# Four attention layers on one core: VectorE's share of the exponentials gets its own storage from the first layer's end on

## The chip, the core and the metric

The kernel runs on one core of a Trainium2 chip. The metric is the device time of one execution in microseconds (us). TensorE (PE) multiplies matrices, ScalarE (ACT) computes exponentials, VectorE (DVE) does elementwise work, GpSimd (POOL) masks and issues some transfers, SyncE (SP) issues the other transfers.

## The reference

Four residual attention layers run one after the other on a 2048 x 640 activation, with 32 heads of 20 columns. Layers 0 and 2 use a causal window of 256 keys; layers 1 and 3 attend to all 2048 keys.

```
def _layernorm(x, axis=-1, eps=1e-5):
    m = jnp.mean(x, axis=axis, keepdims=True)
    v = jnp.var(x, axis=axis, keepdims=True)
    return (x - m) / jnp.sqrt(v + eps)
...
        scores = jnp.einsum("bhqd,bhkd->bhqk", q, k) * (Dh ** -0.5)
        p = _softmax(scores, axis=-1)
        o = jnp.einsum("bhqk,bhkd->bhqd", p, v)
        return (lambda x, *d: x.transpose(*d))(o, 0, 2, 1, 3).reshape(B, S, D) @ wo
...
    x = x + _A_ref(_layernorm(x, axis=-1), A_wqkv, A_wo)
    x = x + _B_ref(_layernorm(x, axis=-1), B_wqkv, B_wo)
    x = x + _A_ref(_layernorm(x, axis=-1), A_wqkv, A_wo)
    x = x + _B_ref(_layernorm(x, axis=-1), B_wqkv, B_wo)
    return x
```

## The kernel before

The 2048 rows are four chunks of 512 (`NC`, `C`), the 32 heads are eight groups of four (`G`). A unit of work, `Unit(l, c, g, part)`, is one layer, one chunk of queries, one group of heads, and in some cases only a part of the keys. A full-attention unit over all keys has 64 banks: one bank is the scores of one head against 128 keys for 512 queries, 128x512 in one PSUM bank. Chunk 0 of layer 1 is cut into four parts of the keys, chunk 0 of layer 3 into two (`PARTS`): a unit of a quarter has 16 banks, a unit of three quarters has 48. Parts exist because the later keys are not yet there: the last chunks of the layer below are still being computed. Their sums wait in `part_o`, the tile `raw_o`, until the last part adds its own (`finish_unit`, L863).

The units stand in one fixed list, `units`, in which layers overlap: windowed units of layer 0 alternate with layer 1's parts 0 to 1, windowed units of layer 2 stand between units of layer 1's chunks 1 to 3 and of layer 3's chunk 0. Part 2 of layer 1's chunk 0 (keys 8 to 12 in units of 128) begins after the last windowed unit of layer 0.

The main loop makes one round (`t`) after the other. A round takes two or three banks from the list (`next_tile`), lets PE write their scores into one of two sets of PSUM banks (L1416), and lets ACT take the exponential of all of them in one instruction (L1442) into one of six `pt` tiles. Two to three rounds later PE multiplies them with the values into the one bank `op` (L1475). At the end of a unit VectorE moves `op` away (`finish_unit`), and the values of the next unit follow.

Everything else, normalisation, projections, output projection, is the background: generators in `todo`, advanced by `background` and `pump` between the rounds. They share one or two PSUM banks (`take_m`), which VectorE empties (`evac`, L334, L339). `keep_clock` fills a round with products of `masks` and `ident` that nobody reads (L315).

VectorE computes some of the exponentials itself. `side_giver` (L932) looks for a full-attention unit among the current and the next two, whose tensors are loaded, and `side_take` (L955) takes two banks off its end. Until chunk 1 of layer 3 a round then holds two banks for ACT and one for VectorE. `side_fixed` (L975) reads that bank into an integer tile `xi`; after two of them, `chain` (L997) computes the exponential of the pair in steps: `fraction` (L1005), `square` (L1013), `cubic` (L1017) and `whole` (L1023), the last two in halves of 512 columns where `HALF` applies. `side_work` emits a step when the planner's own measure of VectorE's backlog, `state["lag"]`, allows it (`WORK_1` 1.4 in layer 1, `WORK` 2.2 later). PE multiplies the result with the values before the unit ends (`side_values`, L1057); at a unit's end `side_ready` can put the end off for up to five rounds, and `side_done` makes what is still missing (`side_push`).

The chain needs two `xi` tiles, one `t` tile and a few tiles for results (`side["out"]`). Before the change there are two periods. `side_early` puts all of them into `raw_o`, when this is free: from layer 1's chunk 1 on, until layer 3 needs `raw_o` again. `side_start` takes three of the five normed-row tiles (`xtp`, tile name `xnT`) and parts of `ka` and `qa` (the windowed layers' keys and queries) after the last windowed unit, from group 4 of layer 3's chunk 0 on. `xnT` holds the transposed normalised rows of one chunk; its other users are the projections.

Of the kernel before, what the change touches and what calls it, by code (L numbers as in the profile page):

```python
# [9 lines left out]
BF16 = mybir.dt.bfloat16  # L10
# [34 lines left out]
PRE_1 = 0.8  # L45
KEEP = 30
HALF = True
HALF_3 = False
MOST_1 = 64
GAP_1 = 5  # L50
QA = 4

# [7 lines left out]
def kernel(  # L60
# [21 lines left out]
    vap = pool("vap", 10)  # L82
    xtp = pool("xtp", 5)
    onp = pool("onp", 2)
# [29 lines left out]
    ka_all = big.tile([P, KA, C], BF16, name="ka", tag="ka")  # L114
    kas = [ka_all[:, n, :] for n in range(KA)]
    qa_all = big.tile([P, QA, C], BF16, name="qa", tag="qa")
    qas = [qa_all[:, n, :] for n in range(QA)]
# [209 lines left out]
    users = {}  # L327

    def used(l, c):
        users[l, c] -= 1  # L330
        if users[l, c] == 0:
            live["xnT"] -= 1

    def evac(out_, in_):  # L334
# [75 lines left out]
    def t_ln(l, c):  # L410
# [18 lines left out]
        )  # L429
        xt = xtp.tile([P, KD, C], BF16, name="xnT", tag="xnT")  # L430

# [431 lines left out]
    def finish_unit(u):  # L863
        l, c, g = u.l, u.c, u.g
        state["lag"] += 0.7
        if u.part and u.part[1] < NT:
            if not part_o:
# [19 lines left out]
        if u.part:  # L887
            nc.vector.tensor_tensor(out=oT, in0=part_o["t"][:, g, :], in1=op, op=ALU.add)
        else:
            nc.vector.tensor_copy(out=oT, in_=op)  # L890
# [8 lines left out]
    side = {  # L899
        "xi": deque(), "chain": deque(), "out": deque(), "late": False, "early": False,  # L900
        "half": None, "at": 0, "last": 0,
    }
    givers = [u for u in units if not u.windowed and (u.l, u.c) != (1, 0)]

    def side_tiles(xi, t, outs):

        side["xi"].extend(xi)
        side["t"] = t
        side["out"].extend(outs)

    def side_start():

        assert live["xnT"] <= 2 and not side["chain"] and side["half"] is None
        tl = [xtp.tile([P, KD, C], BF16, name="xnT", tag="xnT") for _ in range(3)]
        live["xnT"] += 3
        f = [v[:, 0:4, :].rearrange("p a b -> p (a b)").bitcast(F32) for v in tl]
        side["xi"].clear()
        side["out"].clear()
        outs = [ka_all[:, KA - 6 + 2 * n : KA - 4 + 2 * n, :] for n in range(3)]
        outs += [qa_all[:, 2 * n : 2 * n + 2, :] for n in range(2)]  # L920
        side_tiles(f[0:2], f[2].bitcast(F16)[:, 0 : 2 * C], outs)
        side["late"] = True

    def side_early():

        b = part_o["t"]
        f = [b[:, 2 * n : 2 * n + 2, :].rearrange("p a b -> p (a b)") for n in range(2)]
        outs = [b[:, n, :].bitcast(BF16).rearrange("p (a b) -> p a b", a=2) for n in range(5, G)]
        side_tiles(f, b[:, 4, :].bitcast(F16), outs)
        side["early"] = True  # L930

    def side_giver():  # L932

        if not side["late"] and state["tick"] < side["last"] + GAP_1:
            return None
        if side["half"] is not None:
            return side["half"][0]
        if not side["xi"]:
            return None
        while side["at"] < len(givers) and not givers[side["at"]].rest:  # L940
            side["at"] += 1
        for n in range(side["at"], min(side["at"] + 3, len(givers))):
            u = givers[n]
            if id(u) not in loaded or state["tick"] < loaded[id(u)] + 8:
                return None
            if not side["late" if u.l == 3 else "early"]:
                return None
# [49 lines left out]
    def chain(u, xi):  # L997
# [23 lines left out]
        def whole(h):  # L1021
# [5 lines left out]
            if h.stop == 2 * C:  # L1027
                side["xi"].append(xi)
# [28 lines left out]
    def side_values(u, wait):  # L1057

        pairs = side_out.get(id(u), ())
        while u.valued < len(pairs) and pairs[u.valued][1] + wait <= state["tick"]:  # L1060
            pt = pairs[u.valued][0]
            for i in range(2):
# [5 lines left out]
                )  # L1068
            side["out"].append(pt)
            u.valued += 1  # L1070
# [165 lines left out]
    def first_ln():  # L1236

        users[0, 0] = 9
        live["xnT"] += 1
        xt = xtp.tile([P, KD, C], BF16, name="xnT", tag="xnT")  # L1240

# [54 lines left out]
    with tc.manual_schedule():  # L1296
# [74 lines left out]
        while ended is None or t < ended + 8:  # L1371
# [203 lines left out]
```

## Time and profile before

| | us |
|---|---|
| median of three runs | 2171.07 (2169.65 to 2171.41) |
| the profiled execution | 2167.19 |
| its span, first to last instruction | 2165.5 |
| ACT busy | 2086.1 |
| PE busy | 1924.8 |
| VectorE busy | 1488.7 |
| GpSimd busy | 485.9 |
| exponentials on ACT: 128x1536 / 128x1024 | 1280 / 280 instructions |
| banks that VectorE's chain takes (rows of L989) | 210 + 112 = 322 |

The profiled execution took 2167.19 us, 1.7 us more than its span, and 3.9 us less than the median of the three runs. Busy times are sums over the span. PE's busy time holds the unread products too. Stages of the list stand in the span as follows, found from the order of the rounds: layer 1's chunk 0, part 2, from 373.1 to 435.3 us and part 3 to 492.7; chunks 1, 2 and 3 to 744.9, 1005.1 and 1269.1; layer 3's chunk 0, first part, to 1487.7 and second to 1542.6; its chunks 1 to 3 to the end.

### The profile page before, as it was taken

What the parts mean: (1) busy time and instruction counts of PE and PEld (TensorE: products, weight loads), DVE (VectorE), ACT (ScalarE), POOL (GpSimd) and SP (SyncE); (2) the same over time, 40 slices, a digit from 0 to 9 for tenths busy, and PEclk for the clock granted to TensorE, in tenths of its full rate; (3) what the DMA queues carried; (4) which work ended last, traced back from release to release, by engine and by line L of the source; (5) the groups of instructions that cost most, each with busy time, mean ns of one, the idle gap of its engine ahead of it and who ended that gap; (6) DMA issues with size and microseconds to landing.
All of it is one profiled execution on the core that took longest, in us unless ns stands there. A gap on an engine that the chain in (4) does not pass through costs nothing. (4 is left out here: it accounts for less than half of the span.)

```text
span 2165.5 us, 73279 instructions
## 1 busy us (share of the span) xinstructions
PE 1924.8 (89%) x31759; PEld 754.6 (35%) x31759; DVE 1488.7 (69%) x2625; ACT 2086.1 (96%) x1717; POOL 485.9 (22%) x953
## 2 busy tenths in 40 slices
PE   8999999988889898888988989888898898888898
PEld 4444443433333333333333433332332222222222
DVE  5656665426666776776767733676779887888896
ACT  7889899999999999999999999989999999999997
POOL 6665546110122113410053112511000000000000
PEclk9999999999999999999999999999999999999999
DMA  6223233322211323112241133112121111111100
GB/s 204 76 84 107 75 92 101 81 80 64 79 45 27 84 61 90 41 41 61 56 112 33 37 86 99 39 42 77 53 60 44 35 36 42 32 33 39 42 30 17
DMA packets 88418, 137.29 MB, mean 63 GB/s; under 512 B 20766, under 2 KB 63486, under 8 KB 88094
## 3 DMA queue, kind: packets, MB, share of 16 engines
q1 hardware_dynamic: 68878, 79.43, 13.9%
q0 software_dynamic: 19216, 53.17, 8.3%
q8 instruction: 249, 4.08, 0.8%
q14 instruction: 75, 0.61, 0.1%
HBM read 99.52 MB, written 27.79 MB: 59 GB/s over the span
## 5 line engine op out<-in xcount | busy, mean ns | idle before, releaser
L1442 ACT ACTIVATE pt<-ps 128x1536 bf16<-128x1536 f32 (+2 forms) x1641 | 2051.7, 1406 | 46.4 <-PE ps L1416 35.5
L1416 PE MATMUL ps<-qt,kt 32*128 32x512 bf16 x3914 | 544.6, 383 | 59.8 <-ACT pt L1442 52.5
L315 PE MATMUL ps<-masks,ident 128*32 128x512 bf16 x5652 | 505.6, 384 | 96.6 <-ACT pt L1442 47.5
L1475 PE MATMUL ps<-pt,vt 128*21 128x512 bf16 x3774 | 375.9, 386 | 1.8 <-issue 1.0
L1416 PEld LDWEIGHTS <-kt 32*128 32x128 bf16 x3914 | 154.7, 91 | 460.2 <-issue 440.4
L315 PEld LDWEIGHTS <-ident 128*32 128x32 bf16 x5652 | 180.3, 94 | 278.9 <-issue 253.5
L1515 POOL TENSOR_SCALAR_AFFINE_SELECT pt<-pt 128x256 bf16<-128x256 bf16 (+2 forms) x506 | 217.1, 451 | 187.6 <-ACT pt L1442 175.3
L315 PE MATMUL ps<-xnT,wqk 128*32 128x512 bf16 x3320 | 225.2, 381 | 11.9 <-DMA wqk<-in_B_wqkv_dram 2.1
L339 DVE CAST st<-ps 128x512 bf16<-128x512 f32 x134 | 92.5, 690 | 143.9 <-PE ps L315 143.6
L1475 PEld LDWEIGHTS <-vt 128*21 128x21 bf16 x3774 | 93.4, 89 | 260.1 <-issue 256.3
L989 DVE TENSOR_SCALAR xnT<-ps 128x512 int32<-128x512 f32 x210 | 144.1, 687 | 34.6 <-PE ps L971 27.5
L315 PE MATMUL ps<-wop,on 128*32 128x320 bf16 x3712 | 160.5, 300 | 5.7 <-DVE x_sb L587 3.9
L1526 DVE TENSOR_TENSOR pt<-pt,masks 128x256 bf16<-128x256 bf16 (+3 forms) x268 | 113.4, 438 | 46.5 <-ACT pt L1442 44.3
L315 PEld LDWEIGHTS <-on 128*32 128x32 bf16 x5760 | 122.3, 95 | 63.7 <-issue 29.8
L1416 PE MATMUL ps<-qa,ka 32*128 32x384 bf16 (+2 forms) x1408 | 118.0, 276 | 22.5 <-ACT pt L1442 19.1
L587 DVE TENSOR_TENSOR x_sb<-x_sb,ps 128x320 bf16<-128x320 bf16 x120 | 58.2, 485 | 101.6 <-PE ps L315 101.1
L1185 DVE TENSOR_TENSOR on<-on,ps 128x512 bf16<-128x512 bf16 x128 | 86.4, 684 | 59.2 <-PE ps L315 57.0
L315 PE MATMUL ps<-wv,xnT 128*32 128x320 bf16 x2560 | 116.0, 301 | 9.0 <-DVE vs L339 2.0
L315 PEld LDWEIGHTS <-wqk 128*32 128x32 bf16 x3320 | 83.2, 96 | 96.0 <-issue 38.1
L989 DVE TENSOR_SCALAR raw_o<-ps 128x512 int32<-128x512 f32 x112 | 76.8, 686 | 47.3 <-PE ps L1416 46.8
L890 DVE CAST on<-ps 128x512 bf16<-128x512 f32 x112 | 76.7, 685 | 37.9 <-PE ps L1475 30.7
L554 POOL DMA_DIRECT2D k_d<-st x75 | 42.5, 567 | 225.7 <-DVE st L339 213.0
(99 smaller groups left out, 1797.9 us busy)
## 6 DMA issues: line engine op xcount, KB each, us to landing
vt<-v_d SPq DMA_DIRECT2D x48, 336.0 KB
kt<-k_d SPq DMA_DIRECT2D x192, 80.0 KB
wqk<-in_B_wqkv_dram POOLq DMA_DIRECT2D x80, 160.0 KB, 3.5
wqk<-in_A_wqkv_dram POOLq DMA_DIRECT2D x70, 160.0 KB, 3.6
k_d<-st POOLq DMA_DIRECT2D x75, 128.0 KB, 2.5
q_d<-st POOLq DMA_DIRECT2D x75, 128.0 KB, 2.3
qt<-q_d SPq DMA_DIRECT2D x384, 20.0 KB
v_d<-vs POOLq DMA_DIRECT2D x16, 336.0 KB, 3.0
```

What stands on the lines that cost most here:

```text
L315: nc.tensor.matmul(out_[r], lhsT=lhsT[:, r], rhs=rhs, start=start, stop=stop)
L339: nc.vector.tensor_copy(out=out_, in_=in_)
L554: nc.gpsimd.dma_start(out=dst, in_=staging.pop())
L587: nc.vector.tensor_tensor(out=xv, in0=had, in1=yp, op=ALU.add)
L890: nc.vector.tensor_copy(out=oT, in_=op)
L989: nc.vector.tensor_scalar(out=xi.bitcast(I32)[:, i * C : (i + 1) * C], in0=z, scalar1=SCALE * LOG2E * FIX, scalar2=127.5 * FIX, op0=ALU.mu ...
L1185: nc.vector.tensor_tensor(out=oT, in0=oT, in1=zb, op=ALU.mult)
L1416: nc.tensor.matmul(sp[:, i, col * P : (col + qn) * P], lhsT=u.k(kc, j), rhs=u.q(j, q0, qn), start=True, stop=True,)
L1442: nc.scalar.activation(out=pt[:, i:k, b0 * P :], in_=sp[:, i:k, b0 * P :], func=ACT.Exp, scale=SCALE,)
L1475: nc.tensor.matmul(op[32 * j : 32 * j + VW, q0 * P : (q0 + qn) * P], lhsT=u.v(kc, j), rhs=pg[:, i, col * P : (col + qn) * P], start=(first ...
L1515: nc.gpsimd.affine_select(out=v, in_=v, compare_op=ALU.is_gt if later else ALU.is_ge, fill=0.0, base=0, pattern=[[0, k - i], [-1 if later ...
L1526: nc.vector.tensor_tensor(out=pt_[:, i:k, cols], in0=pt_[:, i:k, cols], in1=mv_, op=ALU.mult)
```

## The change

The five normed-row tiles become one tile, `xt_all`, with a list of free places. When part 2 of layer 1's chunk 0 has begun and places 2 to 4 are free, `side_first` keeps these three for the chain for the rest of the kernel: two `xi`, one `t` and two result tiles. Two places are left for normed rows. From the end of layer 1's chunk 0 `raw_o` is lent as eight further result tiles (`side_lend`) and withdrawn when layer 3 begins (`side_retire`, `side_home`); `ka` and `qa` are added after the last windowed unit as before (`side_start`).

The chain therefore no longer pauses between its two periods. Chunk 0 of layer 1 may give banks too (`givers`), in parts 2 and 3, and so may chunk 0 of layer 3 from its first group on. Before chunk 1 of layer 1, a taken bank may follow the last after three rounds (`GAP_0`), not five (`GAP_1`), and the backlog limit there is 2.2, not 1.4. Units of 16 banks may give five rounds after their load (`AFTER`), not eight. The halves of 512 columns apply until `side_start`, not by layer.

```
+AFTER = 5
 HALF = True
+FROM = 2
...
+GAP_0 = 3
...
-    xtp = pool("xtp", 5)
...
+    xt_all = big.tile([P, 5, KD, C], BF16, name="xnT", tag="xnT")
...
+    xt_free = deque(range(5))
+    xt_n = {}
+
+    def take_xt(l, c):
+
+        xt_n[l, c] = xt_free.popleft()
+        return xt_all[:, xt_n[l, c]]
+
     def used(l, c):
         users[l, c] -= 1
         if users[l, c] == 0:
             live["xnT"] -= 1
+            xt_free.append(xt_n.pop((l, c)))
...
-        xt = xtp.tile([P, KD, C], BF16, name="xnT", tag="xnT")
+        xt = take_xt(l, c)
...
             nc.vector.tensor_tensor(out=oT, in0=part_o["t"][:, g, :], in1=op, op=ALU.add)
+            if l == 1 and g == G - 1:
+                side_lend()
...
-    givers = [u for u in units if not u.windowed and (u.l, u.c) != (1, 0)]
...
+    givers = [u for u in units if not u.windowed]
+    away = []
+
+    def side_home(kind, v):
+
+        if any(v is a for a in away):
+            away[:] = [a for a in away if a is not v]
+        else:
+            side[kind].append(v)
+
+    def side_retire(parts):
+
+        for v in parts:
+            for kind in ("xi", "out"):
+                if any(v is a for a in side[kind]):
+                    side[kind] = deque(a for a in side[kind] if a is not v)
+                    break
+            else:
+                away.append(v)
+
+    def side_first():
+
+        for n in range(2, 5):
+            xt_free.remove(n)
+        live["xnT"] += 3
+        f = xt_all[:, 2:5].rearrange("p n a b -> p (n a b)")
+        f = [f[:, n * 2 * C : (n + 1) * 2 * C] for n in range(7)]
+        b = xt_all[:, 2:5].rearrange("p n a b -> p (n a b)")
+        outs = [f[n].rearrange("p (a b) -> p a b", a=2) for n in (5, 6)]
+        side["xi"].extend(b[:, 4 * n * C : 4 * (n + 1) * C].bitcast(F32) for n in range(2))
+        side["t"] = f[4].bitcast(F16)
         side["out"].extend(outs)
+        side["on"] = True
+
+    def side_lend():
+
+        b = part_o["t"]
+        side["lent"] = [b[:, n, :].bitcast(BF16).rearrange("p (a b) -> p a b", a=2) for n in range(G)]
+        side["out"].extend(side["lent"])
 
     def side_start():
 
-        assert live["xnT"] <= 2 and not side["chain"] and side["half"] is None
-        tl = [xtp.tile([P, KD, C], BF16, name="xnT", tag="xnT") for _ in range(3)]
-        live["xnT"] += 3
...
-        side["xi"].clear()
-        side["out"].clear()
         outs = [ka_all[:, KA - 6 + 2 * n : KA - 4 + 2 * n, :] for n in range(3)]
         outs += [qa_all[:, 2 * n : 2 * n + 2, :] for n in range(2)]
-        side_tiles(f[0:2], f[2].bitcast(F16)[:, 0 : 2 * C], outs)
+        side["out"].extend(outs)
         side["late"] = True
 
-    def side_early():
...
     def side_giver():
 
-        if not side["late"] and state["tick"] < side["last"] + GAP_1:
+        gap = GAP_0 if state["unit"] < index[1, 1, 0, None] else GAP_1
+        if not side["late"] and state["tick"] < side["last"] + gap:
             return None
...
-            if id(u) not in loaded or state["tick"] < loaded[id(u)] + 8:
-                return None
-            if not side["late" if u.l == 3 else "early"]:
+            if id(u) not in loaded or state["tick"] < loaded[id(u)] + (AFTER if u.size == 16 else 8):
                 return None
...
-        halves = (slice(0, C), slice(C, 2 * C)) if HALF and (u.l == 1 or HALF_3) else every
+        halves = (slice(0, C), slice(C, 2 * C)) if HALF and not side["late"] else every
...
-            limit = WORK if side["late"] else WORK_1
+            limit = WORK if side["late"] or state["unit"] < index[1, 1, 0, None] else WORK_1
...
-                if not side["early"] and state["unit"] >= index[1, 1, 0, None]:
-                    side_early()
+                if (
+                    not side["on"] and state["unit"] >= index[1, 0, 0, PARTS[1][FROM]]
+                    and all(n in xt_free for n in range(2, 5)) and live["xnT"] <= 2
+                ):
+                    side_first()
+                if side["lent"] and state["unit"] >= index[3, 0, 0, PARTS[3][0]] - BEFORE:
+                    side_retire(side["lent"])
+                    side["lent"] = None
                 if (
                     not side["late"] and state["unit"] >= index[3, 0, 4, PARTS[3][0]]
-                    and live["xnT"] <= 1 and not live["qa"] and not live["ka"]
+                    and not live["qa"] and not live["ka"]
                 ):
                     side_start()
```

More of the change, by code (lines that the diff above doesn't have):

```diff
@@ L46 @@
 KEEP = 30
+AFTER = 5
+THIRD = True
 HALF = True
+FROM = 2
+BEFORE = 0
 HALF_3 = False
@@ L866, in finish_unit @@
         if u.part and u.part[1] < NT:
+            assert l == 1 or side["late"] or not away
             if not part_o:
@@ L899 @@
     side = {
-        "xi": deque(), "chain": deque(), "out": deque(), "late": False, "early": False,
-        "half": None, "at": 0, "last": 0,
-    }
-    givers = [u for u in units if not u.windowed and (u.l, u.c) != (1, 0)]
-    def side_tiles(xi, t, outs):
-        side["xi"].extend(xi)
-        side["t"] = t
-        side["out"].extend(outs)
-    def side_start():
-        assert live["xnT"] <= 2 and not side["chain"] and side["half"] is None
-        tl = [xtp.tile([P, KD, C], BF16, name="xnT", tag="xnT") for _ in range(3)]
-        live["xnT"] += 3
-        f = [v[:, 0:4, :].rearrange("p a b -> p (a b)").bitcast(F32) for v in tl]
-        side["xi"].clear()
-        side["out"].clear()
+        "xi": deque(), "chain": deque(), "out": deque(), "late": False, "on": False,
@@ new lines @@
+        "half": None, "at": 0, "last": 0, "lent": None,
+    }
+    givers = [u for u in units if not u.windowed]
[13 more added lines that the diff above has]
+                away.append(v)
@@ L919, in side_start @@
+    def side_lend():
+        b = part_o["t"]
+        side["lent"] = [b[:, n, :].bitcast(BF16).rearrange("p (a b) -> p a b", a=2) for n in range(G)]
+        side["out"].extend(side["lent"])
+    def side_start():
         outs = [ka_all[:, KA - 6 + 2 * n : KA - 4 + 2 * n, :] for n in range(3)]
         outs += [qa_all[:, 2 * n : 2 * n + 2, :] for n in range(2)]
-        side_tiles(f[0:2], f[2].bitcast(F16)[:, 0 : 2 * C], outs)
+        side["out"].extend(outs)
         side["late"] = True
-    def side_early():
[L926 to L930, printed above, removed]
@@ L937, in side_giver @@
             return side["half"][0]
-        if not side["xi"]:
+        if not side["xi"] or not side["on"]:
             return None
@@ L1027, in whole @@
             if h.stop == 2 * C:
-                side["xi"].append(xi)
+                side_home("xi", xi)
                 side_out.setdefault(id(u), []).append((box["out"], state["tick"]))
         every = (slice(0, 2 * C),)
-        halves = (slice(0, C), slice(C, 2 * C)) if HALF and (u.l == 1 or HALF_3) else every
+        halves = (slice(0, C), slice(C, 2 * C)) if HALF and not side["late"] else every
         cost = 0.7 if len(halves) == 2 else 1.25
@@ L1068, in side_values @@
                 )
-            side["out"].append(pt)
+            side_home("out", pt)
             u.valued += 1
@@ L1239, in first_ln @@
         live["xnT"] += 1
-        xt = xtp.tile([P, KD, C], BF16, name="xnT", tag="xnT")
+        xt = take_xt(0, 0)
         def warm(count):
```

## The prediction

> **What bounds the kernel now.** I read the page's busy shares first, then the groups by form, then the busy times by stage, then a short timeline where ACT waits.
>
> ```profile
> span 2165.5 us, 73279 instructions
> PE 1924.8 (89%) x31759; PEld 754.6 (35%) x31759; DVE 1488.7 (69%) x2625; ACT 2086.1 (96%) x1717; POOL 485.9 (22%) x953
> ```
>
> ACT is busy 96% of the span, VectorE 69%. A kernel like this gains when exponentials leave ACT and the engine that takes them has time where it gets them. Both have to be read by stage:
>
> ```profile
> core 0: us, PE busy (x) PEld busy (x) DVE busy (x) ACT busy (x) POOL busy (x), PEclk, DMA share, GB/s
> 373.10:435.30 62.20, 57.35 (x1043) 25.48 (x1043) 26.89 (x57) 59.15 (x52) 12.72 (x21) 1.00 0.33 79
> 435.30:492.70 57.40, 46.82 (x751) 17.91 (x747) 15.88 (x32) 57.40 (x44) 7.59 (x11) 1.00 0.31 84
> 744.90:1005.10 260.20, 232.00 (x3883) 94.03 (x3883) 186.14 (x351) 258.23 (x205) 63.72 (x119) 1.00 0.24 64
> 1269.10:1399.00 129.90, 113.79 (x2014) 47.67 (x2016) 53.67 (x117) 129.88 (x98) 47.84 (x96) 1.00 0.26 72
> 1399.00:1487.70 88.70, 77.90 (x1253) 31.15 (x1251) 68.76 (x112) 80.30 (x65) 16.17 (x24) 1.00 0.22 59
> 1487.70:1542.60 54.90, 45.39 (x728) 17.06 (x725) 35.77 (x56) 53.39 (x43) 1.64 (x3) 1.00 0.25 66
> ```
>
> The first column after the stretch is its length. The first two rows are parts 2 and 3 of layer 1's chunk 0, the third is chunk 2, the fourth is layer 3's chunk 0 until the chain starts there, the last two are the rest of that chunk. The change fills rows one, two and four. There ACT is idle for 3.05, 0.00 and 0.02 us, and VectorE is 43%, 28% and 41% busy. So these stretches are as long as ACT needs, and VectorE has room. In the stretches where the chain already runs, ACT's idle time is the chain's hidden price: 1.97 us in chunk 2 with 39 banks taken; 8.40 us in the fifth row with 20, and 1.51 in the sixth with 8.
>
> ```profile
> 1444.56 1.21 DVE L1023 SCALAR_TENSOR_TENSOR qa<-xnT,qa 128x1024 uint16<-128x1024 int32 x1
> 1445.91 0.69 DVE L989 TENSOR_SCALAR xnT<-ps 128x512 int32<-128x512 f32 x1
> 1446.52 0.48 DVE L339 CAST vs<-ps 128x320 bf16<-128x320 f32 x1
> 1447.06 0.86 PE L315 MATMUL ps<-wv,xnT 128*32 128x320 bf16 x20 [0.63 <-DVE vs L339]
> 1448.35 1.45 ACT L1442 ACTIVATE pt<-ps 128x1536 bf16<-128x1536 f32 x1 [0.90 <-PE ps L1416]
> ```
>
> Here is how that price arises: a chain step stands ahead of the emptying of a projection's bank on VectorE, the next projection waits 0.63 us for it on PE, the scores stand behind that projection in PE's order, and ACT waits 0.90 us. It happens where the background is heavy, at the end of a windowed layer, and hardly elsewhere.
>
> **What an exponential costs on either side.** Rows of ACT overlap, so their mean of 1524 ns is not the step. The timeline merges 44 full exponentials into one row and eleven alternating ones into another:
>
> ```profile
> 433.98 59.21 ACT L1442 ACTIVATE pt<-ps 128x1536 bf16<-128x1536 f32 x44
> 372.17 12.34 ACT L1442 ACTIVATE pt<-ps 128x1024 bf16<-128x1024 f32 x11
> ```
>
> A full one takes 59.21 / 44 = 1.35 us. The second row is five full and six of 1024 columns: (12.34 - 5 x 1.346) / 6 = 0.94. From start to start, where ACT never waits, the trace has 1.330 and 0.903, so a bank of 512 columns costs ACT 0.427 us. On VectorE a pair of banks costs, by these rows, 2 x 0.687 (L989) + 0.705 + 0.696 + 2 x 0.688 + 2 x 0.684 = 5.5 us in halves, 2.8 us a bank:
>
> ```profile
> L989 DVE TENSOR_SCALAR xnT<-ps 128x512 int32<-128x512 f32 x210 | 144.1, 687 | 34.6 <-PE ps L971 27.5 <-PE ps L1416 4.1
> L1023 DVE SCALAR_TENSOR_TENSOR raw_o<-raw_o 128x512 uint16<-128x512 int32 x112 | 75.2, 684 | 0.0
> L1017 DVE SCALAR_TENSOR_TENSOR raw_o<-raw_o 128x512 f16<-128x512 f16 x112 | 74.3, 688 | 1.1
> L1005 DVE TENSOR_SCALAR raw_o<-raw_o 128x1024 f16<-128x1024 int16 x56 | 39.5, 705 | 0.4
> L1013 DVE TENSOR_TENSOR raw_o<-raw_o 128x1024 f16<-128x1024 f16 x56 | 39.0, 696 | 1.2
> ```
>
> **What the change moves.** In the order of the changed kernel the chain takes 360 banks, not 322: 18 in layer 1's chunk 0 (7 in part 2, 11 in part 3), 114 in the rest of layer 1 (112 before), 46 in layer 3's chunk 0 (28 before: 20 are new ahead of 1399 us, and 26 follow where 28 were), 182 in the last three chunks as before. The number of rounds stays 1612; 41 fewer exponentials have 1536 columns and 43 more have 1024. ACT therefore gives up 38 x 0.427 = 16.2 us. VectorE gets 38 x 2.75 = 105 us more: part 2 goes to (26.9 + 19) / 59 = 78%, part 3 to (15.9 + 30) / 53 = 87%, the stretch to 1399 us to (53.7 + 55) / 121 = 90%. Those shares stand beside 72% in chunk 2 of layer 1.
>
> The price of a new bank, in idle time of ACT that it brings, is not in the trace for these places. The low end is chunk 2's 1.97 / 39 = 0.05 us, the high end the fifth row's 8.40 / 20 = 0.42. I take, by the nearest row: for part 3, with units of 16 banks, the sixth row's 1.51 / 8 = 0.19, so 11 x 0.19 = 2.1; for part 2, with its background, the middle, 7 x 0.24 = 1.7; for the 20 new ones in layer 3, which come every fifth round as in layer 1 but onto a fuller VectorE, 0.12, so 2.4; for layer 1's two, 0.1. In the stretch after 1399 us two banks fewer give back their 0.42 each, which cancels 2 x 0.427 that ACT gets there; this loss is in the 38 already, so I count nothing else.
>
> Unit ends are the new wait. PE's products with the chain's results stand in its order, and the next scores behind them; if the chain isn't done, PE stops. The order has 71 ends with such products, 57 before; at four of them a chain step must be made on the spot, at one before, and 40 rounds put an end off, 10 before. An end put off costs PE nothing by itself, since it goes on with scores and background, and no `pt` tile runs out: a tile's values stand ahead of the scores of the round that writes it anew. A step made on the spot costs at least nothing and at most the longest wait of an exponential on scores in this trace, 1.9 us; three more at 0.55, nearer to the low end because the one before falls in a chunk with little idle time: 1.6.
>
> Two places for normed rows instead of five cost nothing: outside the chain's own tiles never more than two are in use at once in the order of before, so no normalisation moves. Transfers keep their number and order but for small shifts. The tile that replaces the pool adds no waits that would tell on `xnT`; the chain waits for itself as before. PE gets 28 more unread products (seven groups of four), nothing at its rate.
>
> Sum: -16.2 + 2.1 + 1.7 + 2.4 + 0.1 + 1.6 = -8.3 us. The profiled 2167.2 becomes 2158.9; the same step from the median of 2171.07, which is 3.9 above it, gives 2162.8.
>
> The Trainium skill, page SBUF — State Buffer, section Who interferes with whom, says that VectorE's two-port operations, and its operations with two SBUF inputs against GpSimd's reads, block GpSimd for a whole instruction. By that rule a 0.7 us step ahead of the selects of each of the five windowed rounds that now give a bank would make 3.5 us, and the sum -4.8. The trace bears it out weakly, below.
>
> The selects mask the windowed rounds. The first row is from 1353 to 1399 us, with one chain step beside it, the second from 853 to 922, in layer 1's chain:
>
> ```profile
> L1515 POOL TENSOR_SCALAR_AFFINE_SELECT pt<-pt 128x384 bf16<-128x384 bf16 x24 | 13.6, 583 | 8.6 <-ACT pt L1442 8.6
> L1515 POOL TENSOR_SCALAR_AFFINE_SELECT pt<-pt 128x384 bf16<-128x384 bf16 x19 | 11.6, 623 | 6.3 <-ACT pt L1442 6.3
> ```
>
> 40 ns on some 35 selects is 1.4 us, on an engine that waits for ACT in both; it is inside my 0.12 a bank.
>
> **The rivals.** *All of it is gained.* VectorE has the time, and ACT waits nowhere: 2171.1 - 16.2 = 2154.9. For it speaks 0.05 a bank in chunk 2. Against it, VectorE at 87 to 90%, and the fifth row. Chance 0.12.
>
> *Nothing is left.* The background meets the chain everywhere as in the fifth row: 38 x 0.42 = 16.0 comes back, 2171. For it speaks that parts 2 and the first stretch of layer 3 carry a chunk's projections; against it, that in chunk 2 the same projections stood beside the chain for 1.97 us. Chance 0.15 for within 0.2% (4.3 us, about what a measurement of this kernel can tell from no change).
>
> *Unit ends stop PE: slower.* Nine ends in parts 2 and 3 and five in layer 3 get the products anew, on units of 16 banks that last five to six rounds, some 7 us, while one pair's chain needs 5.5 us of VectorE alone. If each costs ACT the longest wait, 14 x 1.9 = 26.6 - 16.2 = 10.4 us slower, 2181.5. It decides from 16.2 / 14 = 1.2 us an end. Against it: the sixth row has five such ends in 1.51 us of idle time, 0.3 each. Chance 0.11.
>
> **How the numbers follow.** My case, a gain of 4.3 to 13 us, has 0.62; with the first rival, faster by over 0.2% has 0.74, within 0.2% 0.15, slower 0.11. The range goes from the full gain, 2154.9, to nothing left and one more forced end of 1.9, 2173.0; all prices at their high ends would be 16.0 + 3 x 1.9 - 16.2 = 5.5 slower, 2176.6, which with the slower rival is left out.
>
> **What would show it.** In the profile after: 360 rows of L989's kind and 323 exponentials of 1024 columns; ACT some 16 us less busy, VectorE some 105 more. Part 2 and part 3 together some 4 us shorter, the stretch of layer 3's chunk 0 up to its second part some 4 to 6 shorter, ACT idle in each by the prices above; chunks 1 to 3 of both layers the same within 2 us. If ACT's idle time grows by 10 us or more, my prices are wrong, and the waits of scores behind projections (background) or behind products with `xnT` and `raw_o` (unit ends) tell which. A time above 2173 would make the mechanism wrong, one under 2154.9 the count of what ACT gives up.

## The result and the profile after

The changed kernel takes 2174.49 us, median of 13 runs (2172.21 to 2181.52), against 2169.86 for the kernel before, 13 runs side by side (2163.77 to 2172.68). The ratio is 1.0032 [1.0022, 1.0042]: slower by 0.3%, 4.6 us by the medians and 7 by the ratio. The forecast was 2162.8, faster, with a range that ended at 2173.0. Time, range and sign were all wrong.

The profiled execution of the changed kernel took 2181.31 us, one of its longest three, so the profiled pair differ by 14.1 us where the medians differ by 4.6. The traces name places; how much each is worth has to come from the runs. The page's busy line and the same stages as before (length, then busy time and instructions by engine, then granted clock):

```profile
span 2179.6 us, 73547 instructions
PE 1943.5 (89%) x31786; PEld 756.5 (35%) x31787; DVE 1585.3 (73%) x2783; ACT 2074.0 (95%) x1719; POOL 493.5 (23%) x959
```
```profile
core 0: us, PE busy (x) PEld busy (x) DVE busy (x) ACT busy (x) POOL busy (x), PEclk, DMA share, GB/s
375.80:445.10 69.30, 65.85 (x1044) 25.53 (x1040) 42.49 (x83) 58.13 (x53) 14.70 (x22) 0.88 0.31 73
445.10:497.00 51.90, 44.72 (x707) 16.82 (x700) 41.83 (x74) 51.90 (x43) 6.24 (x9) 1.00 0.31 84
1276.10:1408.70 132.60, 116.15 (x2018) 48.59 (x2017) 94.59 (x182) 124.87 (x98) 48.80 (x94) 1.00 0.26 71
1408.70:1500.00 91.30, 80.50 (x1323) 32.97 (x1315) 70.25 (x118) 84.17 (x68) 18.32 (x28) 1.00 0.23 60
1500.00:1554.90 54.90, 44.09 (x690) 16.35 (x686) 43.08 (x63) 49.14 (x40) 1.64 (x3) 1.00 0.21 55
```

ACT is 12.1 us less busy and VectorE 96.6 us more: the work has moved. But ACT now waits where it never did. Its idle time (length less ACT's busy time) is 11.17 us in part 2 (3.05 before), 0.00 in part 3, 7.73 in layer 3's chunk 0 up to the old start of the chain (0.02 before), then 7.13 (8.40) and 5.76 (1.51). Part 3 alone did as hoped: 57.4 us became 51.9. Part 2 became 7.1 us longer, partly because PE's granted clock is 0.88 in it. Two stages that the change hardly touches, layer 1's part 0 (no bank given) and chunk 1 (37 banks read in both kernels), are 3.9 and 3.8 us longer; each has a half-clock stretch of 6.8 us, part 0 one of 3.4 us besides, that the profile of before lacks there.

The waits of ACT, longest sums first (what waits <- what it waits for: sum, times, longest; L1456 writes the scores, L1482 is the exponential, L1515 the product with the values):

```profile
ACT pt L1482 <- PE ps L1456: 49.2, 100, 1.4
ACT pt L1482 <- PE ps L1515: 12.6, 11, 2.9
```

The first kind is known from before, where it stands as

```profile
ACT pt L1442 <- PE ps L1416: 35.5, 73, 1.9
```

The second is new: the list of before has no wait of an exponential on value products. An exponential needs nothing that those products make; it waits for them to have read the `pt` tile that it writes anew.

### The profile page after: what moved, and what is told of

It is laid out like the page before. It is cut to its first block, busy times and chain, and to the rows that moved or that the text cites. A ratio compares the mean times of both kernels' runs of the same rounds, so it can differ in the third digit from the quotient of the medians.

```text
span 2179.6 us, 73547 instructions
## 1 busy us (share of the span) xinstructions
PE 1943.5 (89%) x31786; PEld 756.5 (35%) x31787; DVE 1585.3 (73%) x2783; ACT 2074.0 (95%) x1719; POOL 493.5 (23%) x959
## 5 line engine op out<-in xcount | busy, mean ns | idle before, releaser
L1482 ACT ACTIVATE pt<-ps 128x1536 bf16<-128x1536 f32 (+3 forms) x1643 | 2039.5, 1379 | 73.9 <-PE ps L1456 49.2
L320 PE MATMUL ps<-masks,ident 128*32 128x512 bf16 x5680 | 512.4, 388 | 102.8 <-ACT pt L1482 51.9
L1456 PE MATMUL ps<-qt,kt 32*128 32x512 bf16 x3914 | 554.4, 386 | 51.3 <-ACT pt L1482 46.3
L1515 PE MATMUL ps<-pt,vt 128*21 128x512 bf16 x3736 | 373.1, 387 | 2.3 <-ACT pt L1482 1.3
L1456 PEld LDWEIGHTS <-kt 32*128 32x128 bf16 x3914 | 151.3, 91 | 454.9 <-issue 438.0
L1023 DVE TENSOR_SCALAR xnT<-ps 128x512 int32<-128x512 f32 x360 | 247.4, 687 | 84.7 <-PE ps L1456 49.0
L1555 POOL TENSOR_SCALAR_AFFINE_SELECT pt<-pt 128x128 bf16<-128x128 bf16 (+2 forms) x512 | 223.2, 458 | 175.5 <-ACT pt L1482 164.2
L1515 PEld LDWEIGHTS <-vt 128*21 128x21 bf16 x3736 | 92.2, 89 | 255.5 <-issue 252.5
L1566 DVE TENSOR_TENSOR pt<-pt,masks 128x512 bf16<-128x512 bf16 (+4 forms) x272 | 114.8, 439 | 33.9 <-ACT pt L1482 32.7
L1456 PE MATMUL ps<-qa,ka 32*128 32x384 bf16 (+2 forms) x1408 | 120.3, 276 | 19.9 <-ACT pt L1482 16.5
L1039 DVE TENSOR_SCALAR xnT<-xnT 128x1024 f16<-128x1024 int16 x180 | 125.6, 698 | 3.8
```

The lines of the kernel that those rows point to most:

```text
L320: nc.tensor.matmul(out_[r], lhsT=lhsT[:, r], rhs=rhs, start=start, stop=stop)
L1023: nc.vector.tensor_scalar(out=xi.bitcast(I32)[:, i * C : (i + 1) * C], in0=z, scalar1=SCALE * LOG2E * FIX, scalar2=127.5 * FIX, op0=ALU.mu ...
L1039: V.tensor_scalar(out=t[:, h], in0=low[:, h], scalar1=T1, scalar2=T0, op0=ALU.mult, op1=ALU.add)
L1456: nc.tensor.matmul(sp[:, i, col * P : (col + qn) * P], lhsT=u.k(kc, j), rhs=u.q(j, q0, qn), start=True, stop=True,)
L1482: nc.scalar.activation(out=pt[:, i:k, b0 * P :], in_=sp[:, i:k, b0 * P :], func=ACT.Exp, scale=SCALE,)
L1515: nc.tensor.matmul(op[32 * j : 32 * j + VW, q0 * P : (q0 + qn) * P], lhsT=u.v(kc, j), rhs=pg[:, i, col * P : (col + qn) * P], start=(first ...
```

## The experiments

Every kernel below ran in 12 executions (x9_from3 11, x11_fill 6) beside the kernel before. "Banks" counts what the chain takes. "At one clock" is the mean time brought to a mean granted clock of 0.996 with 1.2 us for each 0.001; that slope is the one over 111 executions of the kernel before, whose clock varies from 0.992 to 0.999 by itself. Within single kernels the slope lies between 0.7 and 1.4, so differences of a microsecond in the last column mean little.

| kernel | banks | median us | ratio to before | mean clock | at one clock |
|---|---|---|---|---|---|
| before (with b_again) | 322 | 2168.4 | 1 | 0.9964 | 2169.3 |
| after | 360 | 2174.5 | 1.0032 [1.0022, 1.0042] | 0.9945 | 2174.2 |
| b_again | 322 | 2169.25 | 1.0008 [0.9996, 1.0021] | 0.9962 | |
| x3_neither | 328 | 2168.91 | 1.0003 [0.9993, 1.0013] | 0.9962 | 2169.5 |
| x1_no_first | 344 | 2172.83 | 1.0021 [1.0012, 1.0030] | 0.9938 | 2170.2 |
| x2_no_layer3_early | 348 | 2172.35 | 1.0020 [1.0006, 1.0033] | 0.9938 | 2170.3 |
| x5_pt7 | 360 | 2169.47 | 1.0006 [0.9995, 1.0017] | 0.9943 | 2167.6 |
| x7_before_pt7 | 322 | 2169.75 | 1.0008 [0.9999, 1.0018] | 0.9963 | 2170.0 |
| x8_quiet | 338 | 2167.22 | 1.0001 [0.9991, 1.0012] | 0.9951 | 2166.9 |
| x6_quiet_pt7 | 338 | 2161.00 | 0.9971 [0.9961, 0.9981] | 0.9957 | 2161.4 |
| x10_pt7_no3 | 348 | 2166.08 | 0.9989 [0.9978, 1.0000] | 0.9956 | 2165.9 |
| x9_from3 | 350 | 2171.45 | 1.0018 [1.0008, 1.0029] | 0.9929 | 2168.5 |
| x11_fill | 360 | 2177.39 | 1.0039 [1.0025, 1.0053] | 0.9953 | 2175.8 |
| x12_quiet_pt7_fill | 338 | 2162.06 | 0.9971 [0.9959, 0.9982] | 0.9971 | 2163.8 |

The theories after the first look: (A) the six `pt` tiles run out where a unit's end is put off ("unit-end theory" in the expectations); (B) a bank costs more than I took where the background is busy ("background theory"); (C) the lower clock explains the loss ("clock theory"). Some expectations below place the half-clock stretch at 365 to 382 us; in the profile of after it lies from 375.2 to 392.3, and in those of x5_pt7 and x10_pt7_no3 from 372 to 389.

**The kernel before once more, and the change without its parts.** `b_again` is the kernel before, unchanged.

> The kernel before, unchanged, for the granted clock of each of its executions. Clock theory, as a property of the change: the clock stays at 0.998 in all, with times within 0.2%. Clock as a property of the execution alone: values from 0.990 to 0.998 occur here too, and the slower executions are those with the lower clock.

No difference shows. Slower executions are mostly those with a lower clock (one of 2175.63 us at 0.996 is an exception), and the profiled one has half-clock stretches of 6.8 us at 88 and 372 us: the kernel before has them too. At a clock of exactly 0.996 the medians are 2168.6 (26 executions of before) and 2173.0 (5 of after). So 4.4 us of the loss stand without any difference in clock. The means of the clock, 0.9964 and 0.9945, make 1.9 x 1.2, some 2 us, the rest of the 7.

`x1_no_first`: the chain starts with layer 1's chunk 1.

```
-                    not side["on"] and state["unit"] >= index[1, 0, 0, PARTS[1][FROM]]
+                    not side["on"] and state["unit"] >= index[1, 1, 0, None]
```


> The changed kernel with the chain's start moved from part 2 of layer 1's chunk 0 to chunk 1, so chunk 0 of layer 1 gives no bank (344 banks, not 360); the rest is the changed kernel. Unit-end theory (the chain's late results put unit ends off, the six pt tiles run out, and exponentials wait for value products): only one of the eleven such waits, 0.7 us, lies in chunk 0 of layer 1, so ACT gets 7.7 us back and loses little: 3 to 6 us slower than the changed kernel, ratio to before about 1.005. Background theory (chain steps stand ahead of the emptying of projection banks wherever the background is heavy): part 2 goes back from 14.2 us of stall to 5.1, so within 2 us of the changed kernel. Clock theory (the chain in part 2 makes TensorE fall to half clock, as in the profiled execution from 365 to 382 us): the half-clock stretch at part 2 is gone in this kernel and it is 4 to 8 us faster than the changed one in its slower executions.

`x2_no_layer3_early`: layer 3 gives nothing until the last windowed unit is done.

```
+        if u.l == 3 and not side["late"]:
+            return None
         if u.l == 1 and len(u.aside) >= MOST_1:
```


> The changed kernel, but units of layer 3 give no bank until the last windowed unit is done, as before the change (348 banks; 18 in layer 1's chunk 0 stay). Unit-end theory: the two waits at the second unit of layer 3 (0.5 and 2.9 us) and the ends behind them go, those after 1399 us stay: 2 to 4 us faster than the changed kernel. Background theory: the stretch before the start goes from 11.3 us of stall back to 1.6, against 8.5 us that ACT gets again: within 2 us of the changed kernel. Forecast theory (a new bank costs 0.12 there): 5 to 6 us slower than the changed kernel.

`x3_neither`: both edits, so that the new storage is left, with the rules that go with it.

> The changed kernel with both new stretches off: no bank before chunk 1 of layer 1, and none in layer 3 before the last windowed unit is done (328 banks, 6 more than before, four of them in the units of 16 banks of layer 3). What is left is the new storage: one tile for the normed rows with two places left, raw_o as result tiles. Background and unit-end theories: the storage costs nothing, ratio to before 0.999 to 1.001. If the two places for normed rows or the one tile cost something, it shows here as 3 us or more.

No cost of the storage shows (1.0003), though the six more banks, worth 2.6 us, bring nothing either; the profile of x3_neither has 2.8 us of waits on value products. Each half of the change alone makes the kernel slower, by 3.9 and 3.4 us from x3_neither's median, though 16 and 20 more banks leave ACT, worth 6.8 and 8.5 us. Both together make 5.6. So neither half is the culprit alone: new banks cost about what they bring in both places. At one clock the two are 0.7 and 0.8 us above x3_neither, which is (6.8 + 0.7) / 16 = 0.47 us a bank for layer 3's early ones and (8.5 + 0.8) / 20 = 0.47 for layer 1's first. Both together are 4.7 above it, some 3 us more than the two halves make; why, these runs do not show.

Of the expectations, the unit-end theory missed x1_no_first (1.7 us faster than after by the medians, not 3 to 6 slower), where the background theory's "within 2 us" came true by the medians and not at one clock (4.0). For x2_no_layer3_early the unit-end theory's 2 to 4 us were right (2.1 by the medians, 3.9 at one clock), and the forecast's price of 0.12 a bank, by which it would have been 5 to 6 us slower, was not. Of the clock theory it came true that x1_no_first's slowest execution is below after's, by 6.8 us; but its profile still has a half-clock stretch at 372 us, of 6.8 us, and its mean clock is lower than after's, 0.9938.

x2_no_layer3_early also gives part 2 without the half clock, and early layer 3 without new banks:

```profile
372.70:435.60 62.90, 58.76 (x1040) 25.23 (x1040) 42.17 (x83) 57.23 (x54) 14.70 (x22) 1.00 0.34 81
1265.40:1397.10 131.70, 114.85 (x2054) 48.79 (x2057) 54.53 (x117) 130.80 (x98) 47.72 (x97) 1.00 0.26 71
```

Part 2 then has 62.90 - 57.23 = 5.67 us of idle time with the chain, 3.05 without it: 2.62 / 7 = 0.37 us a bank. Of after's 11.17 the other half, 5.5 us, goes with the half clock.

What makes the price in part 2 is not what the prediction's timeline showed. PE waits there for the emptying of a background bank for 0.2 us in all, in x2_no_layer3_early as in before, though ACT's waits for scores grow from 2.6 us in 4 places to 4.9 in 10. But PE is busy for 58.76 of 62.90 us, 93% (57.35 of 62.20, 92%, before), where in part 3, which costs nothing, it is busy for 44.72 of 51.90, 86%. So the scores in part 2 may simply stand behind PE's own work; no run tests that.

**The `pt` tiles.** The place of the longest new wait in the profile of after (the timeline: start, length, engine, line; in brackets the wait and for whom). L1057 is the chain's last step, L1099 the product with the chain's result:

```profile
1325.72 0.40 PE L1515 MATMUL ps<-pt,vt 128*21 128x512 bf16 x4
1325.92 1.28 DVE L1057 SCALAR_TENSOR_TENSOR xnT<-xnT 128x512 uint16<-128x512 int32 x2
...
1326.66 0.38 PE L1099 MATMUL ps<-xnT,vt 128*21 128x512 bf16 x1 [0.54 <-DVE xnT L1057]
1327.26 0.38 PE L1099 MATMUL ps<-xnT,vt 128*21 128x512 bf16 x1 [0.23 <-DVE xnT L1057]
1328.25 0.39 PE L1456 MATMUL ps<-qt,kt 32*128 32x512 bf16 x3
1329.71 0.39 PE L1456 MATMUL ps<-qt,kt 32*128 32x512 bf16 x3
1330.04 0.61 PE L1515 MATMUL ps<-pt,vt 128*21 128x512 bf16 x8
1330.53 1.45 ACT L1482 ACTIVATE pt<-ps 128x1536 bf16<-128x1536 f32 x1 [2.86 <-PE ps L1515]
```

It reads like this. The unit's end has been put off, and its last two chain steps are now made on the spot (1325.92). Only after the products with their result (1326.66, 1327.26) can the unit end, and only then may PE multiply the next unit's first banks with the values: `op` is one bank. Those banks have stood in a `pt` tile since six rounds before. The exponential at 1330.53 writes that tile, and its round's scores stand ahead of the products that free it. The values usually follow two to three rounds behind, so with six tiles an end put off by three rounds or more uses them up. The order of after has 40 rounds that put an end off (10 before); ACT waits in this way 11 times, twice for over 2 us, and nearly all of it, 11 of the 12.6 us, in layer 3's chunk 0.

`x5_pt7` gives the changed kernel a seventh tile; two small pools lose a tile each for the room.

```
-    ptp = pool("ptp", 6)
-    stp = pool("stp", 4)
+    ptp = pool("ptp", 7)
+    stp = pool("stp", 3)
...
-    lnp = pool("lnp", 4)
+    lnp = pool("lnp", 3)
```


> The changed kernel with seven pt tiles for six; the room comes from one staging tile (three, not four) and one set of normalisation statistics (three, not four). The chain's banks are the same 360 in the same rounds. Unit-end theory: the waits of exponentials on value products, 12.7 us in 11 places in the changed kernel's profile, fall to a third or less, and the time by 5 to 9 us, to below the kernel before (ratio 0.996 to 0.999). Background and clock theories: no change, ratio to before 1.002 to 1.004.

The wait on the value products falls from 12.6 us to 0.8, and the time by 5.0 us by the medians, 6.6 at one clock: the low end of what the unit-end theory said, though not "to below the kernel before" (1.0006). The known wait stays (first row):

```profile
ACT pt L1482 <- PE ps L1456: 47.4, 100, 1.4
ACT pt L1482 <- PE ps L1515: 0.8, 3, 0.3
```

So does the half clock, 17.1 us of it from 372.4: (A) and (C) are separate. `x7_before_pt7` does the same to the kernel before.

> The kernel before with seven pt tiles, three staging tiles and three sets of statistics. Unit-end theory: the profile before has no wait of an exponential on value products, so nothing is gained, ratio 0.999 to 1.001; any loss is the price of the smaller pools. If pt tiles were short in the kernel before as well, or if the seventh tile helped otherwise, it would be 3 us or more faster, and x5_pt7 would show nothing about the change.

Nothing is gained there (1.0008): the seventh tile is worth something only where ends are put off. That is (A), shown. But 360 banks with seven tiles only equal 322 with six, where ACT has 16.2 us less to do. Early layer 3 stays nearly as dear as with six tiles (length 131.80, ACT 124.95, so 6.85 us idle; 6.85 / 20 = 0.34 a bank):

```profile
1269.40:1401.20 131.80, 116.15 (x2018) 48.49 (x2017) 94.55 (x182) 124.95 (x98) 49.10 (x94) 1.00 0.26 71
```

Here the prediction's mechanism shows in part. In this stretch ACT waits 6.0 us for scores in 12 places, where the list of before has none, and PE's waits for VectorE to empty a background bank grow from 2.2 us in 8 places to 5.4 in 14. But in x2_no_layer3_early, which gives no bank here, such waits of PE are 4.0 us in 10 places, and ACT waits only 0.9 us for scores. So the price is measured, and its cause is in part argued.

**Banks only where the background is quiet.** `x8_quiet` keeps six tiles, and lets layer 1's chunk 0, and layer 3's until `side_start`, give a bank only while no background is waiting:

```
         if not side["xi"] or not side["on"]:
             return None
+        if todo and not side["late"] and (
+            state["unit"] < index[1, 1, 0, None] or state["unit"] >= index[3, 0, 0, PARTS[3][0]]
+        ):
+            return None
```


> The changed kernel, with one condition more: in chunk 0 of layer 1 and, until the last windowed unit is done, of layer 3, a new bank is taken only while no background task is pending (338 banks: 22 fewer than the changed kernel, 16 more than before). Background theory (in those two places a chain step stands ahead of the emptying of projection banks): the banks that cost more than the 0.427 us they bring are the ones left out, the 16 others cost 0.1, so 16 x 0.33 = 5 us faster than before, ratio 0.997 to 0.999, and 7 to 10 us faster than the changed kernel. Unit-end theory alone: the waits on value products fall with the put-off ends, from 40 to 24: from 12.7 to 6 or 7 us, against 9 us that ACT gets again, so no faster than the changed kernel, ratio 1.002 to 1.004.

With 22 banks fewer than after, it is 7.3 us faster and level with before (1.0001). So the unit-end theory alone is out; of the background theory's two numbers, 7 to 10 us faster than after came true and 5 us faster than before did not. Some of the 7.3 is (A) again, fewer ends put off: the wait on value products is 6.6 us in six places. `x6_quiet_pt7` adds the seventh tile.

> The same condition, and seven pt tiles for six, with three staging tiles and three sets of statistics as in x5_pt7. Background and unit-end theories together: no wait of an exponential on value products over 1 us is left, 2 to 5 us faster than x8_quiet, ratio to before 0.995 to 0.998, the fastest so far. If only one of the two mechanisms were at work, it would equal x5_pt7 or x8_quiet.

This version beats both kernels: 0.9971 [0.9961, 0.9981], 6.3 us faster than before by the ratio. Its 16 banks more than before are worth 16 x 0.427 = 6.8 us, so here nearly all that ACT gives up reaches the end. The stages show why (the same three as above: part 2, part 3, early layer 3):

```profile
373.70:435.50 61.80, 58.62 (x1049) 25.56 (x1046) 32.32 (x67) 59.77 (x53) 14.05 (x22) 1.00 0.33 82
435.50:489.20 53.70, 45.74 (x720) 17.39 (x723) 29.69 (x55) 53.70 (x43) 6.27 (x10) 1.00 0.31 88
1267.10:1395.90 128.80, 113.94 (x2022) 47.88 (x2021) 61.67 (x129) 128.79 (x98) 48.48 (x96) 1.00 0.26 72
```

ACT is idle for 2.03, 0.00 and 0.01 us, no more than before the change, and the stages are 0.4, 3.7 and 1.1 us shorter. The exponentials wait for scores as long as in before, and hardly for value products:

```profile
ACT pt L1486 <- PE ps L1460: 35.4, 69, 2.8
ACT pt L1486 <- PE ps L1519: 0.7, 3, 0.3
```

The condition also makes the banks fewer: early layer 3 reads 5 where after reads 17, part 3 six where after reads ten. No run leaves out as many banks without regard to the background, so "quiet" and "fewer" are not told apart by the total. For "quiet" speaks part 3, where after takes all its banks and ACT's idle time is 0.00.

From x8 to x6 the seventh tile alone is worth 6.2 us by the medians, 5.5 at one clock. `x10_pt7_no3` separates what is left: seven tiles, every bank in layer 1's chunk 0, none early in layer 3.

> x2_no_layer3_early (units of layer 3 give nothing before the last windowed unit is done, 348 banks) with seven pt tiles, three staging tiles and three sets of statistics. Unit-end theory: x2's 7.5 us of waits on value products go, 4 to 6 us faster than x2, ratio to before 0.998 to 1.000. Background theory: what is then left of chunk 0 of layer 1 shows its own price: 18 banks bring ACT 7.7 us, and if part 2 costs 8 us of stall, the time equals the kernel before; the forecast's price of 0.2 a bank would give 5 us faster than before.

At 348 banks it is 0.9989 [0.9978, 1.0000]. Against x5_pt7 it lacks 12 banks, worth 5.1 us, and is not slower but faster, by 3.4 us by the medians and 1.6 at one clock: early banks in layer 3 bring nothing, rather a loss, with seven tiles too, so that (A) is not all, and a price as in (B) stands beside it. Against x6_quiet_pt7 it has ten banks more and is 4.5 us slower at one clock.

**Part 2 or part 3, and the clock.** `x9_from3` starts the chain with part 3, with six tiles.

```
-FROM = 2
+FROM = 3
```


> The changed kernel with the chain's start at part 3 of layer 1's chunk 0, not part 2 (350 banks: none in part 2, 6 in part 3, 54 instead of 46 from layer 3's chunk 0 on less what its later units give). Background theory: part 2 goes back to 5 us of stall from 7.8 (without a half-clock stretch) or 14 (with it), ACT gets 4 us again: within 2 us of the changed kernel at the same granted clock. Clock theory (the chain in part 2 lengthens the half-clock stretch near 365 us from 6.8 to 17.1 us): no stretch over 6.8 us there, mean clock back near 0.996, and 3 to 6 us faster than the changed kernel.

Its 350 banks are 6 in part 3, 112 in the rest of layer 1, 50 in layer 3's chunk 0 (the expectation says 54) and 182. It is slower than before, 1.0018, with 9.2 us of waits on value products, and has the lowest clock of all, 0.9929, without any chain in part 2. So the lower clock is not a matter of part 2 alone, and the clock theory's 0.996 did not come. At one clock, however, it is 5.7 us faster than after, not within 2 us as the background theory had it: by this the banks of part 2 cost more than they bring, even if 3.4 us of the 5.7 are the fewer waits on value products. Why that is more than the 0.37 us a bank in part 2's idle time is not explained.

`x11_fill` and `x12_quiet_pt7_fill` add unread products to after and to x6_quiet_pt7, from the last groups of layer 0 to the end of layer 1's chunk 0:

```
-            state["least"] = (1.76 if state["unit"] >= woven else 1.0) * n_b / 3
+            full_rate = 2.4 if index[0, 3, 4, None] <= state["unit"] < index[1, 1, 0, None] else 1.76
+            state["least"] = (full_rate if state["unit"] >= woven else 1.0) * n_b / 3
```


> The changed kernel with more unread products from the last groups of layer 0 to the end of layer 1's chunk 0: the least that keep_clock fills a round up to is 2.4, not 1.76, 38 groups of four more. Clock theory (too little work on TensorE there lets the clock fall): no half-clock stretch near 365 us, mean clock above 0.995, 3 to 6 us faster than the changed kernel. If the stretch comes from elsewhere: it stays, and the time is the same or up to 4 us longer, for the products that stand ahead of scores.

> x6_quiet_pt7, the fastest so far, with the same additional unread products (37 groups of four). Clock theory: one to two us faster than x6, ratio to before 0.996; otherwise the same or slower by up to 4 us.

Neither profile has a half-clock stretch in part 2 (after's has, x6_quiet_pt7's had none either), and the mean clock is higher (0.9953 and 0.9971 for 0.9945 and 0.9957), but neither kernel is faster, and x11_fill has its 12.6 us of waits on value products in eleven places again. Whether the products took what the clock gave, these two runs can't say. Against (C) as the main cause stand the 4.4 us that are left at a clock of exactly 0.996, and x11_fill, which has a higher clock than after and all of (A) and is no faster (1.0039 [1.0025, 1.0053]).

## Why the prediction was wrong

**What failed first: "no `pt` tile runs out: a tile's values stand ahead of the scores of the round that writes it anew".** That holds while the value products follow two to three rounds behind. An end put off adds its rounds to that, and the sentence is then false: at 1330 us the tile's values stand behind the scores of the very round that writes it. I had counted the 40 put-off rounds and not set them against six tiles. The term at nothing measured 12.6 us in the trace of after, and 5.0 to 6.6 us of time, by x5_pt7.

**The rival on the slower side named the place, not the means.** It had PE stopped by chain steps at 14 new unit ends, deciding from 1.2 us an end. The measured waits, shared out over these ends, are 12.6 / 14 = 0.9 us an end, through the tiles and ACT; I had 1.6 us in all, as steps made on the spot. At 0.9 it does not make the kernel slower alone; with the background's price it does.

**The background's prices were low.** In early layer 3 I took 0.12 us a bank, nearer to chunk 2's 0.05 than to the 0.42 of the stretch that follows. After shows (7.73 - 0.02) / 20 = 0.39, of which 3.3 us are waits on value products, and seven tiles still 0.34; 17 of the 20 banks are read inside this stretch, so a bank costs rather more than that. The nearest row was the next stretch, as full of background, and not chunk 2. Part 2 at 0.24 was 0.37 without the half clock, and not by the mechanism I had (above). Part 3 at 0.19 was nothing: PE and the background have more room there, ACT's idle time is 0.00, and the 5.5 us gained there are the whole of 11 banks at 0.427 and a little more. The rule that x6_quiet_pt7 follows, banks where the queue is empty, fits these three prices.

**After 1399 us I counted nothing.** ACT's idle time there went from 9.91 to 7.13 + 5.76 = 12.89, with 7.7 us of it on value products. Without these it would have fallen, and in x5_pt7, with hardly any, it is 6.20 + 2.05 = 8.25.

**The clock was not in the sum.** Part 2's half clock of 17.1 us costs 4.6 us of ACT in the profiled execution, but on the mean of the runs the whole difference in clock is some 2 us.

**Of the signs named in advance, one kind of wait was missing.** "If ACT's idle time grows by 10 us or more, my prices are wrong": it grew by 8.1 in part 2 (5.5 of it with the half clock), 7.7 in early layer 3 and 3.0 after it. Parts 2 and 3 together were to be 4 us shorter and are 1.6 us longer; layer 3's chunk 0 up to its second part was to be 4 to 6 us shorter and is 5.3 us longer (132.6 + 91.3 for 129.9 + 88.7). The waits to look at were named as scores behind projections and products with `xnT`; the third kind, an exponential behind value products, was not.

**What was right.** 360 rows of the step that reads a bank, and 323 exponentials of 1024 columns, as forecast; ACT's busy time fell by 12.1 of 16.2, and VectorE's rose by 96.6 of 105:

```profile
L1482 ACT ACTIVATE pt<-ps 128x1024 bf16<-128x1024 f32 x323 | 342.9, 1067 | 18.0 <-PE ps L1456 14.4 <-PE ps L1515 2.8
L1023 DVE TENSOR_SCALAR xnT<-ps 128x512 int32<-128x512 f32 x360 | 247.4, 687 | 84.7 <-PE ps L1456 49.0 <-PE ps L1005 30.9 <-issue 0.8
```

Two places for normed rows, and the storage, cost nothing that shows (x3_neither). The worth of a bank, 0.427 us, holds where little waits: x6_quiet_pt7 gains 6.3 us on 16 banks.

**The selects.** In 1362 to 1408 us of after, beside the chain, a masking select takes (from the groups by form):

```profile
L1555 POOL TENSOR_SCALAR_AFFINE_SELECT pt<-pt 128x384 bf16<-128x384 bf16 x17 | 10.9, 652 | 5.0 <-ACT pt L1482 5.0
```

It was 583 ns in the corresponding stretch before. The Trainium skill's rule, page SBUF — State Buffer, section Who interferes with whom, that such VectorE operations, issued first, block GpSimd for a whole instruction, is borne out in direction: 69 ns a select, some 2.4 us on 35. GpSimd still waits for ACT there (5.0 us), so that is no term of its own.

**What stays open.** At one clock x5_pt7 is 1.7 us faster than before. Its banks are worth 16.2, and the prices measured in part 2 (2.6) and early layer 3 (6.8) leave 6.8. That is about 5 us of loss that idle time in these two stages does not hold. Some 3.4 us of it stand in ACT's busy time, which fell by 2086.1 - 2073.3 = 12.8 us in x5_pt7's profile, not by 16.2. An exponential of 1536 columns that begins after a wait takes 1.45 us (the row at 1330.53), in a row without waits 1.35, so each new wait costs more than its idle time. The rest is not located. Nor is it known why kernels with the added chain get a lower clock on the mean, or what makes part 2 so dear.

## What to carry over

When a consumer is put off, whatever it frees late has to be covered: count the tiles in flight at the longest delay, not at the usual one, and look for the producer waiting on the reads of its own output buffer. When work moves to an engine that is only partly idle, try giving it that work while its queue is empty; with a seventh tile, the 16 banks taken in that way were worth nearly all that ACT gave up, where 38 taken everywhere with six tiles were worth less than nothing. Price such work by the row that has the same neighbours, even if another row has the same pattern.

## What the runs showed of the hardware

PE's granted clock falls to half in stretches of 3.4, 6.8, 10.2 or 17.1 us, all near multiples of 3.4, in the kernel before too. Many lie near 88, 215 and 372 us, but no place has one in every profile, and the kernel before has 6.8 us near 372 in b_again and none there in its first profile. The longest, of 17.1 us, appears in part 2 in the profiles of after, x5_pt7 and x10_pt7_no3. After with it, and x2_no_layer3_early in as long a time at full clock:

```profile
375.20:392.30 17.10, 17.10 (x178) 4.08 (x177) 7.45 (x15) 12.13 (x11) 3.42 (x6) 0.50 0.13 31
```
```profile
372.10:389.20 17.10, 16.19 (x300) 6.93 (x297) 11.49 (x23) 16.76 (x16) 3.38 (x6) 1.00 0.15 38
```

PE makes 178 products where it makes 300, and ACT is busy for 12.13 us, not 16.76: 4.6 us lost. That agrees with the slope over the runs of before: 17.1 us at half clock lower the mean of a 2180 us span by 0.004, which at 1.2 us for each 0.001 is 4.7. The Trainium skill, page TensorE: Matmul & The Clock Gate, section HAM oscillation — how this bites in real kernels, has idle gaps of PE over some 3.4 us bring on the half clock. The length of the stretches fits that window, the cause doesn't: in the ten microseconds ahead of this one PE is busy for 8.36, and its longest wait there is 1.0 us.
